# Cluster-masked attention: centroid products in four column tiles, one-hot rows made on two engines and moved by four transfers, two weight loads moved

## Chip, cores and metric

The kernel runs on one core of one Trainium2 chip. The metric is the device time in microseconds (us), the median of three runs. TensorE is called PE, VectorE DVE, ScalarE ACT, GpSimd POOL and SyncE SP, as in the profile.

## What is computed

Attention in which a query sees only the keys of its own cluster, followed by two mixture-of-experts layers (8 experts, width 512, hidden 1024, 1536 tokens). The change touches the attention alone, and two loads of the first layer's weights.

```python
B, H, S, D = 2, 8, 768, 64; n_clusters = 16
q_assign = argmax(q_n @ c_n^T); k_assign = argmax(k_n @ c_n^T)     # normed rows and centroids
mask = q_assign[:, :, :, None] == k_assign[:, :, None, :]
scores = scale * np.matmul(q, k.transpose(0, 1, 3, 2))
scores = np.where(mask, scores, -1000000000.0)
attn = np.exp(scores - max); attn = attn / (sum + 1e-09)
x = np.matmul(attn, v); x = moe(x); return moe2(x)
```

## The kernel before, in words

**Tiling.** Heads are worked two at a time: two batches with four head pairs each are eight "pairs", numbered 0 to 7. A pair has 12 chunks: six blocks of 128 queries for each of its two heads (j). Each chunk is a slot of the main loop, numbered 0 to 11 in its pair.

**Scores and mask.** q and k are split into a rounded part and a rest (qh, ql, kh, kl; scale folded into q), and the products run in a rounded 32-bit form. The first operands x1, y1 hold qh over ql and kh twice; the second, x2, y2, hold qh and kl in 64 rows, and from row 64 on 16 one-hot rows of the cluster of each query (values 0, 1) and of each key (values -2^100, 0). So the second product adds 0 where the clusters agree and -2^100 where they don't. The second operands stand in two sets, for even and odd pairs.

**A slot** issues, in this order: four products into a score tile pss (L238; two such tiles), its row maximum nm on DVE (L246), the six transposes ppt of the chunk two back (L268) in two tiles of three, copied to pt by ACT and DVE (L270); what is due of the products with v (av, L280, slots 10, 0, 4 and 6; px, the norm and the gate's lp at slots 1 and 7, L307 to L323); a step of preparation for the next pair; a step of other work; the exponential pe on ACT with its sum (L254). The instructions of an engine run in the order in which this loop issues them. The tiles ppt, plog, plt, poh, px and pws (products for the first layer's weight scales) share a pool of three PSUM banks.

**Preparation of the next pair** is a list of nine steps, one a slot: qh on ACT; ql on DVE, kh on ACT and kl on POOL; the products of q and k with the centroids (plog: two halves of 384 columns, each in two column tiles for q and k; lt, one half copied by ACT, one by DVE); six transposes plt; the row maximum and eq on DVE, times a rank on POOL, and the twelve transfers of operands by SP; first (m and oh on DVE: the first cluster that reaches the maximum); two empty steps; oh_t: two tiles of three transposes poh, two DVE operations that scale and shift into ot, and four SP transfers into x2 and y2. For pair 0 the list begins at slot 2, so that oh_t falls on slot 9. The q, k and v of the pair after next are loaded by SP at slots 7, 8 and 9.

**EARLY** is a table that hangs steps of the first expert layer on slots of pairs 6 (-2) and 7 (-1): "load" is a 1 MB transfer of raw weights, "piece" a step that casts them (wh on ACT L840, wl on DVE L847).

Of the kernel before, what the change touches and what calls it, by code (L numbers as in the profile page):

```python
# [15 lines left out]
BIG = float(2.0 ** 100)  # L16
WARM = 8
P0 = 2
LD = {7: "q", 8: "k", 9: "v"}
WARM2 = 6  # L20


# [6 lines left out]
def attention(tc, end, ps_t, ident, wu, q, k, v, centroids, wg, x_half, lg_sb, consts, before_half, after_half, extra, slot):  # L29


    nc = tc.nc
# [10 lines left out]
    with ExitStack() as ctx:  # L43
# [11 lines left out]
        def cpy(dst, src):  # L55
            nc.sync.dma_start(dst.bitcast(F32), src.bitcast(F32))

        def centroid_norms():

            nc.vector.tensor_tensor(c_sq, cw, cw, op=ALU.mult)  # L60
            p = ps_t.tile([P, 512], F32, tag="t", name="pc")[:64, :NP]
            for hp in range(NP):
                for t in range(2):
                    nc.tensor.matmul(p[32 * t:32 * t + 2 * G, hp:hp + 1], c_sq[:, hp].rearrange("p j g -> p (j g)"),
                                     ones, start=True, stop=True)
            nc.scalar.sqrt(c_n, p)
            nc.vector.tensor_scalar_add(c_n, c_n, 1e-6)
            nc.vector.reciprocal(c_n, c_n)
# [5 lines left out]
        def zero_rows(s):  # L74
            for j in range(2):
                for nm in ("x2", "y2"):
                    nc.gpsimd.memset(xs[nm, s, j][64:128].bitcast(F32), 0.0)
# [8 lines left out]
        def gate_loads(wgv):  # L86
            for j in range(2):
# [2 lines left out]

        cw = one.tile([P, NP, 2, G], F32, name="cw")
        c_sq = one.tile([P, NP, 2, G], F32, name="c_sq")
        c_n = one.tile([64, NP], F32, name="c_n")
        ones = one.tile([P, 1], F32, name="a_ones")
        rev = one.tile([P, G], F32, name="rev")
        msc = one.tile([64, 2], F32, name="msc")
        rw = end.tile([P, NP, P + 2 * E], F32, name="rw")
        xs = {(nm, s, j): one.tile([P, S], F32R, name=f"{nm}_{s}{j}")
              for s in range(2) for j in range(2) for nm in ("x2", "y2")}

        warm0 = one.tile([1, 1], F32, name="warm0")
        st = {}
# [41 lines left out]
            cpy(xs["y2", s, j][:D], d["kl"][r])  # L144

        def logits(pi):
            b, hp = pairs[pi]
            d = st[pi]
            d["lt"] = lt = w1.tile([64, S], F32, tag="lt", name="lt")
            for hf in range(2):  # L150
                p = ps_t.tile([P, 512], F32, tag="t", name="plog")[:64, :W]
                for t, nm in enumerate("qk"):
                    nc.tensor.matmul(p[32 * t:32 * t + 2 * G], cw[:, hp].rearrange("p j g -> p (j g)"),
                                     d[nm][:, hf * W:(hf + 1) * W], start=True, stop=True)
                if hf == 0:
                    nc.scalar.mul(lt[:, :W], p, c_n[:, hp:hp + 1])
                elif pi == 0:
                    nc.scalar.mul(lt[:, W:], p, c_n[:, hp:hp + 1])
                else:
                    nc.vector.tensor_scalar_mul(lt[:, W:], p, c_n[:, hp:hp + 1])  # L160

        def logits_t(pi):
            d = st[pi]
            p = ps_t.tile([P, 512], F32, tag="t", name="plt")[:, :C * 4 * G]
            d["lg"] = p.rearrange("p (c t j g) -> p c t j g", c=C, t=2, j=2)
            for c in range(C):
                nc.tensor.transpose(p[:, c * 4 * G:(c + 1) * 4 * G], d["lt"][:, c * P:(c + 1) * P], ident[:64, :64])
# [18 lines left out]

        def oh_t(pi):
            d = st[pi]
            ot = w1.tile([64, S], F32R, tag="lt", name="ot")
            ohv = d["oh"].rearrange("p (c i) g -> p c (i g)", i=4)  # L190
            for hf in range(2):
                p = ps_t.tile([P, 512], F32, tag="t", name="poh")[:64, :W]
                for c in range(HALF):
                    nc.tensor.transpose(p[:, c * P:(c + 1) * P], ohv[:, hf * HALF + c], ident)
                nc.vector.tensor_scalar(ot[:, hf * W:(hf + 1) * W], p, msc[:, 0:1], msc[:, 1:2],
                                        op0=ALU.mult, op1=ALU.add)
            s = pi % 2
            for j in range(2):
                cpy(xs["x2", s, j][64:64 + G], ot[j * G:(j + 1) * G])
                cpy(xs["y2", s, j][64:64 + G], ot[(2 + j) * G:(3 + j) * G])  # L200

        def first_mask(j):

# [15 lines left out]
        def first_rows(j):  # L219
            for hf in range(2):  # L220
                p = ps_t.tile([P, 512], F32, tag="t", name="poh")[:64, :W]
                for c in range(HALF):
                    nc.tensor.transpose(p[:, c * P:(c + 1) * P],
                                        oh0[j][:, hf * HALF + c].rearrange("p t g -> p (t g)"), ident)
                hs = slice(hf * W, (hf + 1) * W)
                nc.scalar.copy(xs["x2", 0, j][64:64 + G, hs], p[:G])
                nc.vector.tensor_scalar(xs["y2", 0, j][64:64 + G, hs], p[2 * G:3 * G], BIG, -BIG,
                                        op0=ALU.mult, op1=ALU.add)
# [117 lines left out]
        def last():  # L346
# [1 line left out]
            yield from after_half(B - 1, 1, rows)  # L348

        prep = [  # L350
            lambda i: part(i, "qh"),
            lambda i: (part(i, "ql"), part(i, "kh"), part(i, "kl")),
            lambda i: logits(i),
            lambda i: logits_t(i),
            lambda i: (argmax(i), operands(i, 0), operands(i, 1)),
            lambda i: first(i),
            lambda i: None,
            lambda i: None,
            lambda i: oh_t(i),
# [16 lines left out]
        zero_rows(0)  # L376
        for j in range(2):
            nc.gpsimd.memset(oh0[j], 0.0)
        for (p0, c0, x) in ((0, 0, 1.0), (0, 1, 0.0), (32, 0, BIG), (32, 1, -BIG)):
            nc.vector.memset(msc[p0:p0 + 32, c0:c0 + 1], x)  # L380
        keep_warm(WARM)
        part(0, "qh")
        centroid_norms()
# [46 lines left out]
        for i in range(len(seq) + LAG + 1):  # L430
# [15 lines left out]
            if cur:  # L446
                pi = cur[0]
                sl = i % n
                if sl in LD:
                    load(pi + 2, LD[sl])  # L450
                if i == 0:
                    for _ in masks[1]:
                        pass
                if i == 1:
                    first_rows(1)
                ps = sl - P0 + (sl - P0 > 6) if pi == 0 else sl
                if pi + 1 < NPR and 0 <= ps < len(prep):
# [267 lines left out]
class MoE:  # L725
# [353 lines left out]
    def run(self, task):  # L1079
# [3 lines left out]
        for i, u in enumerate(units):  # L1083
# [888 lines left out]
```

## Time and profile before

| | us |
|---|---|
| runs | 616.56, 616.71, 619.94; median 616.71 |
| profiled execution | 615.39 |
| its span | 613.5 |
| PE busy | 565.1 (92%) |
| DVE busy | 466.1 (76%) |
| ACT busy | 421.3 (69%) |
| POOL busy | 215.4 (35%) |

The profile shows one execution. Its time is 1.9 us above the span, which reaches from the first to the last instruction. A PE row's duration is modelled, and rows overlap; the distance from one start to the next says how long the work takes. Pair 0 begins at 12.70 us, pair 1 at 41.39, pair 7 at 234.40; the attention's last products are done by about 288, and the rest is the two expert layers.

### The profile page before, as it was taken

To read this page: it belongs to the slowest core of one execution; us is meant where nothing else is said; L and a number is where in the kernel's file an instruction comes from. 1 tells how busy PE (TensorE), PEld (TensorE's weight loads), DVE (VectorE), ACT (ScalarE), POOL (GpSimd) and SP (SyncE) were. 2 spreads that over 40 slices of the span, in tenths; PEclk is the share of its full clock that TensorE was granted. 3 is DMA by queue.
4 is the path that set the end of the run, shared out by engine and by line. 5 is a ranking of instruction groups with operands and counts; after the bars stand their busy time and mean duration, and the time that the engine had idled before them with its cause. 6 is when DMAs were issued, how large, how long until landed. Compare 5 with 4: busy or idle time off the path is not lost.

```text
span 613.5 us, 14527 instructions
## 1 busy us (share of the span) xinstructions
PE 565.1 (92%) x5428; PEld 466.1 (76%) x5428; DVE 466.1 (76%) x1186; ACT 421.3 (69%) x901; POOL 215.4 (35%) x426
## 2 busy tenths in 40 slices
PE   6899999998999998988899999997998999999993
PEld 2666767676767676657778998996887988999992
DVE  5867686778989676868586788789778666989881
ACT  4766666776676668963585787875864576969781
POOL 8702020202341110115634355624624523263441
PEclk9899999999999999999899999999999999999997
DMA  5879482747409881522466765976973657999930
GB/s 145 212 217 283 123 176 88 169 110 153 146 22 241 247 242 35 178 70 107 150 219 236 244 208 201 306 246 194 326 234 89 235 181 245 316 305 312 318 114 21
DMA packets 75920, 117.55 MB, mean 192 GB/s; under 512 B 10906, under 2 KB 43802, under 8 KB 75843
## 3 DMA queue, kind: packets, MB, share of 16 engines
q1 hardware_dynamic: 72419, 106.76, 58.3%
q0 software_dynamic: 3264, 9.72, 4.7%
q8 instruction: 45, 0.74, 0.5%
q14 instruction: 32, 0.26, 0.1%
q10 hardware_dynamic: 160, 0.07, 0.0%
HBM read 84.28 MB, written 12.87 MB: 158 GB/s over the span
## 4 chain that ended last, share of the span: by engine, by line
PE 61%; DVE 17%; ACT 12%; issue 4%; DMA 3%; SPq 1%; ACTq 0%; POOL 0%; DVEq 0%
PE ph L950 15%; PE py L1025 13%; PE av L280 9%; PE pss L238 7%; PE ppt L268 6%; PE pz L1000 3%; DVE nm L246 3%; DVE wl L847 3%; ACT wh L840 3%; ACT pe L254 2%; PE pyo L1646 2%; PE pxt L927 2%; ACT pt L270 1%; ACT xo L1700 1%; DVE hl L962 1%
## 5 line engine op out<-in xcount | busy, mean ns | idle before, releaser
L847 DVE SCALAR_TENSOR_TENSOR wl<-raw,sw,wh 128x1024 f16<-128x1024 f32 x128 | 163.5, 1284 | 17.9 <-ACT wh L840 16.8
L840 ACT ACTIVATE wh<-raw,sw 128x1024 f16<-128x1024 f32 x128 | 146.0, 1148 | 2.5 <-DMA x<-ot 2.4
L246 DVE TENSOR_REDUCE nm<-pss 128x1 f32<-128x768 f32 x96 | 91.5, 953 | 41.2 <-PE pss L238 37.6
L254 ACT ACTIVATE pe<-pss,nm 128x768 f32<-128x768 f32 x96 | 87.1, 907 | 24.2 <-DVE nm L246 24.2
L950 PEld LDWEIGHTS <-wh 128*128 128x128 f16 x1152 | 87.7, 99 | 15.4 <-issue 10.9
L238 PE MATMUL pss<-y,x 128*128 128x384 f32 x384 | 93.6, 365 | 4.8 <-ACT pe L254 3.2
L268 PE MATMUL ppt<-ident,pe 128*128 128x128 f32 x576 | 80.4, 275 | 3.3 <-ACT pt L270 1.4
L238 PEld LDWEIGHTS pss<-y,x 128*128 128x128 f32 x384 | 63.2, 190 | 25.2 <-issue 13.2
L270 ACT COPY pt<-ppt 128x384 f32<-128x384 f32 x128 | 57.9, 482 | 29.4 <-PE ppt L268 29.1
L268 PEld LDWEIGHTS ppt<-ident,pe 128*128 128x128 f32 x576 | 69.2, 142 | 8.9 <-ACT pt L270 2.3
L1025 PEld LDWEIGHTS <-wh 128*128 128x128 f16 x960 | 73.2, 100 | 3.4
L950 PE MATMUL ph<-xh,wh 128*128 128x192 f16 (+14 forms) x576 | 67.2, 240 | 8.6 <-DVE hl L962 6.2
L280 PE MATMUL av<-pt,v 128*64 128x384 f32 x384 | 68.8, 494 | 0.0
L950 PE MATMUL ph<-xl,wh 128*128 128x192 f16 (+14 forms) x576 | 67.3, 240 | 0.2 <-issue 0.2
L950 PE MATMUL ph<-xh,wl 128*128 128x192 f16 (+14 forms) x576 | 67.3, 240 | 0.0
L952 ACT ACTIVATE hh<-ph 128x128 f16<-128x128 f32 (+14 forms) x144 | 44.5, 315 | 27.1 <-PE ph L950 25.8
L962 DVE SCALAR_TENSOR_TENSOR hl<-ph,hh 128x192 f16<-128x192 f32 (+14 forms) x127 | 41.1, 336 | 24.4 <-ACT hh L952 22.8
L1025 PE MATMUL py<-hh,wh 128*128 128x192 f16 (+13 forms) x480 | 47.3, 241 | 0.5 <-ACT hh L952 0.3
L1025 PE MATMUL py<-hl,wh 128*128 128x192 f16 (+13 forms) x480 | 46.9, 240 | 0.2 <-DVE hl L962 0.2
L950 PEld LDWEIGHTS <-wl 128*128 128x128 f16 x576 | 45.5, 99 | 1.9
L1025 PE MATMUL py<-hh,wl 128*128 128x192 f16 (+13 forms) x480 | 46.7, 241 | 0.0
L280 PEld LDWEIGHTS av<-pt,v 128*64 128x64 f32 x384 | 24.8, 136 | 28.4 <-issue 28.1
(326 smaller groups left out, 865.3 us busy)
## 6 DMA issues: line engine op xcount, KB each, us to landing
raw<-in_moe_w SPq DMA_DIRECT2D x64, 1024.0 KB, 5.9
y<-kh SPq DMA_DIRECT2D x31, 192.0 KB, 4.0
x<-qh SPq DMA_DIRECT2D x30, 192.0 KB, 4.6
q<-in_q SPq DMA_DIRECT2D x8, 384.0 KB, 4.8
k<-in_k SPq DMA_DIRECT2D x8, 384.0 KB, 5.0
x<-ql SPq DMA_DIRECT2D x16, 192.0 KB, 3.3
v<-in_v SPq DMA_DIRECT2D x8, 384.0 KB
out<-zt SPq DMA_DIRECT2D x1, 3072.0 KB
```

The lines of the kernel that those rows point to most:

```text
L238: nc.tensor.matmul(p[:, hf, :W], xx[:, c * P:(c + 1) * P], yy[:, hf * W:(hf + 1) * W], start=a, stop=o)
L246: nc.vector.tensor_reduce(nm, p[:, :, :W], axis=AX.XY, op=ALU.max, negate=True)
L254: nc.scalar.activation(pe, p[:, :, :W], AF.Exp, bias=d["nm", c, j], scale=1.0, accum_out=d["sm"][:, c, j:j + 1])
L268: nc.tensor.transpose(p[:, kc * P:(kc + 1) * P], pe[:, kh, kc * P:(kc + 1) * P], ident)
L270: eng(pt[:, kh * HALF:(kh + 1) * HALF, (c % HALF) * P:(c % HALF + 1) * P], p.rearrange("p (a b) -> p a b", a=HALF))
L280: nc.tensor.matmul(p[j * D:(j + 1) * D, :W], d["v"][:, j, kc, :], d["pt", hf, j][:, kc, :], start=(kc == 0), stop=(kc == C - 1))
L840: nc.scalar.activation(hi[:, :, s], x[:, :, s], AF.Copy, scale=sw)
L847: nc.vector.scalar_tensor_tensor(lo[:, :, s], x[:, :, s], sw, hi[:, :, s], op0=ALU.mult, op1=ALU.subtract, accum_out=fl)
L950: nc.tensor.matmul(p[:, :N], w[:, c, fs], x[:, c, :N], start=(k == 0), stop=(k == 11))
L952: nc.scalar.activation(hh[:, f, :N], p[:, :N], AF.Relu)
L962: nc.vector.scalar_tensor_tensor(hl[:, f, :N], p[:, :N], 0.0, hh[:, f, :N], op0=ALU.max, op1=ALU.subtract)
L1025: nc.tensor.matmul(p[:, :N], w[:, f, s], x[:, f, :N], start=(k == 0), stop=(k == 23))
```

## The change

1. **plog** is one tile of 128 partitions: q and k, first and second half, in four column tiles; lt is one operation, on DVE (ACT for pair 0). plt is three transposes of 128 rows instead of six of 64, and so is poh.
2. **The rows.** DVE makes oa (both kinds of rows, two heads' worth of partitions), and POOL multiplies it twice by a factor 0 or 1 for each partition (own) into ot, so that rows of the other head are zero for k. x2 and y2 of both heads are one tile, and each of the four transfers fills 32 rows of both heads: oa for x2 goes to both heads, ot to y2.
3. **Steps.** Preparation has eight steps: logits at slot 0; plt and qh; argmax, kh and kl; ql; first and the operands' transfers; two empty; oh_t at slot 7 (slot 9 for pair 0, as before). The loads of q and k stand behind oh_t in the same slot, v one slot later.
4. **EARLY.** The third and fourth load of raw weights move from slots 4 and 6 of pair 6 to slots 8 and 10. At the start, the memsets of msc move from DVE (four) to POOL (eight), and DVE sums the identity into own.

```diff
-LD = {7: "q", 8: "k", 9: "v"}
+LD = {7: "qk", 8: "v"}
...
-                for t in range(2):
+                for t in range(4):
                     nc.tensor.matmul(p[32 * t:32 * t + 2 * G, hp:hp + 1], c_sq[:, hp].rearrange("p j g -> p (j g)"),
                                      ones, start=True, stop=True)
...
-        xs = {(nm, s, j): one.tile([P, S], F32R, name=f"{nm}_{s}{j}")
-              for s in range(2) for j in range(2) for nm in ("x2", "y2")}
+        xs2 = {(nm, s): one.tile([P, 2, S], F32R, name=f"{nm}_{s}") for s in range(2) for nm in ("x2", "y2")}
+        xs = {(nm, s, j): t[:, j] for (nm, s), t in xs2.items() for j in range(2)}
...
         def logits(pi):
-            d["lt"] = lt = w1.tile([64, S], F32, tag="lt", name="lt")
+            d["lt"] = lt = w1.tile([P, W], F32, tag="lt", name="lt")
+            p = ps_t.tile([P, 512], F32, tag="t", name="plog")[:, :W]
             for hf in range(2):
-                p = ps_t.tile([P, 512], F32, tag="t", name="plog")[:64, :W]
                 for t, nm in enumerate("qk"):
-                    nc.tensor.matmul(p[32 * t:32 * t + 2 * G], cw[:, hp].rearrange("p j g -> p (j g)"),
+                    r = 64 * hf + 32 * t
+                    nc.tensor.matmul(p[r:r + 2 * G], cw[:, hp].rearrange("p j g -> p (j g)"),
                                      d[nm][:, hf * W:(hf + 1) * W], start=True, stop=True)
-                if hf == 0:
-                    nc.scalar.mul(lt[:, :W], p, c_n[:, hp:hp + 1])
-                elif pi == 0:
-                    nc.scalar.mul(lt[:, W:], p, c_n[:, hp:hp + 1])
-                else:
-                    nc.vector.tensor_scalar_mul(lt[:, W:], p, c_n[:, hp:hp + 1])
+            if pi == 0:
+                nc.scalar.mul(lt, p, c_n[:, hp:hp + 1])
+            else:
+                nc.vector.tensor_scalar_mul(lt, p, c_n[:, hp:hp + 1])
...
-            for c in range(C):
-                nc.tensor.transpose(p[:, c * 4 * G:(c + 1) * 4 * G], d["lt"][:, c * P:(c + 1) * P], ident[:64, :64])
+            for c in range(HALF):
+                nc.tensor.transpose(p[:, c * P:(c + 1) * P], d["lt"][:, c * P:(c + 1) * P], ident)
...
         def oh_t(pi):
             d = st[pi]
-            ot = w1.tile([64, S], F32R, tag="lt", name="ot")
-            ohv = d["oh"].rearrange("p (c i) g -> p c (i g)", i=4)
+            oa = w1.tile([P, W], F32R, tag="lt", name="oa")
+            ot = w1.tile([P, 2, W], F32R, tag="ot", name="ot")
+            ohv = d["oh"].rearrange("p (c i) g -> p c (i g)", i=8)
+            p = ps_t.tile([P, 512], F32, tag="t", name="poh")[:, :W]
+            for c in range(HALF):
+                nc.tensor.transpose(p[:, c * P:(c + 1) * P], ohv[:, c], ident)
+            nc.vector.tensor_scalar(oa, p, msc[:, 0:1], msc[:, 1:2], op0=ALU.mult, op1=ALU.add)
+            for j in range(2):
+                nc.gpsimd.tensor_scalar(ot[:, j], oa.bitcast(F32), own[:, j:j + 1], None, op0=ALU.mult)
+            s = pi % 2
             for hf in range(2):
-                p = ps_t.tile([P, 512], F32, tag="t", name="poh")[:64, :W]
-                for c in range(HALF):
-                    nc.tensor.transpose(p[:, c * P:(c + 1) * P], ohv[:, hf * HALF + c], ident)
-                nc.vector.tensor_scalar(ot[:, hf * W:(hf + 1) * W], p, msc[:, 0:1], msc[:, 1:2],
-                                        op0=ALU.mult, op1=ALU.add)
-            s = pi % 2
-            for j in range(2):
-                cpy(xs["x2", s, j][64:64 + G], ot[j * G:(j + 1) * G])
-                cpy(xs["y2", s, j][64:64 + G], ot[(2 + j) * G:(3 + j) * G])
+                cpy(xs2["x2", s][64:96, :, hf * W:(hf + 1) * W],
+                    oa[64 * hf:64 * hf + 32].unsqueeze(1).to_broadcast([32, 2, W]))
+            for hf in range(2):
+                cpy(xs2["y2", s][64:96, :, hf * W:(hf + 1) * W], ot[64 * hf + 32:64 * hf + 64])
...
         prep = [
-            lambda i: part(i, "qh"),
-            lambda i: (part(i, "ql"), part(i, "kh"), part(i, "kl")),
             lambda i: logits(i),
-            lambda i: logits_t(i),
-            lambda i: (argmax(i), operands(i, 0), operands(i, 1)),
-            lambda i: first(i),
+            lambda i: (logits_t(i), part(i, "qh")),
+            lambda i: (argmax(i), part(i, "kh"), part(i, "kl")),
+            lambda i: part(i, "ql"),
+            lambda i: (first(i), operands(i, 0), operands(i, 1)),
             lambda i: None,
             lambda i: None,
             lambda i: oh_t(i),
...
+        for j in range(2):
+            nc.vector.tensor_reduce(own[:, j:j + 1], ident.rearrange("p (a i g) -> p a i g", i=2, g=G)[:, :, j],
+                                    axis=AX.XY, op=ALU.add)
...
-                if sl in LD:
-                    load(pi + 2, LD[sl])
...
-                ps = sl - P0 + (sl - P0 > 6) if pi == 0 else sl
+                ps = sl - P0 if pi == 0 else sl
                 if pi + 1 < NPR and 0 <= ps < len(prep):
                     prep[ps](pi + 1)
+                for nm in LD.get(ps, ()):
+                    load(pi + 2, nm)
...
-         (-2, 4): ('load',),
-         (-2, 6): ('load',),
+         (-2, 8): ('load',),
          (-2, 9): ('open_ring', 'open_first', 'piece'),
-         (-2, 10): ('gather',),
+         (-2, 10): ('gather', 'load'),
```

Three places show how instructions move; the names are the program's tiles. First SP's queue at the end of pair 1, where the transfers of the second operands (x2 and y2 of the odd set, before x_10, x_11, y_10, y_11, after x_1 and y_1) and the loads stand. Before:

```order
L56 DMA y_1221<-kh 64x768 x2
L56 DMA x_1220<-ql 64x768
L56 DMA x_11_171<-qh 64x768
L56 DMA y_11_172<-kl 64x768
L1400 DMA wsm<-in_moe_w 128x8x64
L114 DMA q<-in_q 128x768
L114 DMA k<-in_k 128x768
L56 DMA x_10_169<-ot 16x768
L56 DMA y_10_170<-ot 16x768
L56 DMA x_11_171<-ot 16x768
L56 DMA y_11_172<-ot 16x768
L111 DMA v<-in_v 128x768
```

and after the change:

```order
L56 DMA x_1211<-qh 64x768
L56 DMA y_1212<-kh 64x768 x2
L56 DMA x_1211<-ql 64x768
L56 DMA x_1_168<-qh 64x768
L56 DMA y_1_169<-kl 64x768
L1408 DMA wsm<-in_moe_w 128x8x64
L56 DMA x_1_168<-oa 32x2x384 x2
L56 DMA y_1_169<-ot 32x2x384 x2
L115 DMA q<-in_q 128x768
L115 DMA k<-in_k 128x768
L112 DMA v<-in_v 128x768
```

The loads of q and k stood ahead of the rows' transfers and now stand behind them.

Second, DVE's queue in slots 1 to 4 of pair 1, from the norm's ri on (after the change from the end of slot 0). Before:

```order
L295 TENSOR_SCALAR ri<-sm 128x6
L296 RECIPROCAL ri<-ri 128x6
L315 TENSOR_TENSOR lp<-px,ri 128x48
L323 TENSOR_TENSOR x<-px,ri 128x3x128
L124 SCALAR_TENSOR_TENSOR ql<-q,qh 128x768
L246 TENSOR_REDUCE nm<-pss 128x1
L270 COPY pt_762<-ppt 128x3x128
L160 TENSOR_SCALAR lt<-plog,c_n 64x384
L246 TENSOR_REDUCE nm<-pss 128x1
L270 COPY pt_791<-ppt 128x3x128
L246 TENSOR_REDUCE nm<-pss 128x1
L270 COPY pt_762<-ppt 128x3x128
```

and after:

```order
L161 TENSOR_SCALAR lt<-plog,c_n 128x384
L252 TENSOR_REDUCE nm<-pss 128x1
L301 TENSOR_SCALAR ri<-sm 128x6
L302 RECIPROCAL ri<-ri 128x6
L321 TENSOR_TENSOR lp<-px,ri 128x48
L329 TENSOR_TENSOR x<-px,ri 128x3x128
L252 TENSOR_REDUCE nm<-pss 128x1
L276 COPY pt_766<-ppt 128x3x128
L176 TENSOR_REDUCE mx<-plt 128x24
L178 TENSOR_TENSOR eq<-plt,mx 128x384
L252 TENSOR_REDUCE nm<-pss 128x1
L276 COPY pt_795<-ppt 128x3x128
```

lt has moved ahead of nm of slot 1, mx and eq from slot 4 to slot 2, and ql from slot 1 to slot 3.

Third, ACT's queue from the end of pair 0's last products to slot 4 of pair 1. Before:

```order
L270 COPY pt_950<-ppt 128x3x128 x2
L287 COPY avo<-av_1024 128x384
L122 ACTIVATE qh<-q 128x768
L254 ACTIVATE pe,sm<-pss,nm 128x768
L270 COPY pt_992<-ppt 128x3x128 x2
L126 CAST kh<-k 128x768
L254 ACTIVATE pe,sm<-pss,nm 128x768
L270 COPY pt_1127<-ppt 128x3x128
L156 ACTIVATE lt<-plog,c_n 64x384
L254 ACTIVATE pe,sm<-pss,nm 128x768
L270 COPY pt_1163<-ppt 128x3x128
L254 ACTIVATE pe,sm<-pss,nm 128x768
```

and after:

```order
L276 COPY pt_959<-ppt 128x3x128 x2
L293 COPY avo<-av_1016 128x384
L260 ACTIVATE pe,sm<-pss,nm 128x768
L276 COPY pt_986<-ppt 128x3x128 x2
L123 ACTIVATE qh<-q 128x768
L260 ACTIVATE pe,sm<-pss,nm 128x768
L276 COPY pt_1124<-ppt 128x3x128
L127 CAST kh<-k 128x768
L260 ACTIVATE pe,sm<-pss,nm 128x768
L276 COPY pt_1160<-ppt 128x3x128
L260 ACTIVATE pe,sm<-pss,nm 128x768
L276 COPY pt_1124<-ppt 128x3x128
```

qh has moved from slot 0 into slot 1 and kh from slot 1 into slot 2; ACT's half of lt is gone.

## Rows read from the trace of the kernel before

**Rows 1.** Busy time by stretch, pair 1: us, PE, PEld, DVE, ACT, POOL, clock, DMA.
```profile
41.39:72.12 30.73, 30.38 (x203) 22.00 (x202) 22.05 (x40) 20.47 (x45) 3.61 (x6) 1.00 0.78 220
```

**Rows 2.** PE's timeline in pair 1: start, duration, operation, count; stretches of one kind joined.
```profile
45.02 0.97 PE L238 MATMUL pss<-y,x 128*128 128x384 f32 x4
...
47.29 0.97 PE L238 MATMUL pss<-y,x 128*128 128x384 f32 x4
48.10 0.82 PE L268 MATMUL ppt<-ident,pe 128*128 128x128 f32 x6
48.84 0.51 PE L153 MATMUL plog<-q,cw 128*32 128x384 f32 x1
...
50.81 0.97 PE L238 MATMUL pss<-y,x 128*128 128x384 f32 x4
...
52.88 0.97 PE L238 MATMUL pss<-y,x 128*128 128x384 f32 x4
...
56.52 0.97 PE L238 MATMUL pss<-y,x 128*128 128x384 f32 x4
...
57.90 0.96 PE L238 MATMUL pss<-y,x 128*128 128x384 f32 x4
...
61.52 0.97 PE L238 MATMUL pss<-y,x 128*128 128x384 f32 x4
...
63.63 0.96 PE L238 MATMUL pss<-y,x 128*128 128x384 f32 x4
```

**Rows 3.** Groups by line and form, 41.39 to 234.4 us: busy us, mean ns, idle before.
```profile
L246 DVE TENSOR_REDUCE nm<-pss 128x1 f32<-128x768 f32 x73 | 69.6, 953 | 33.4 <-PE pss L238 30.4 <-ACT pe L254 1.9 <-ACT qh L122 0.8
L254 ACT ACTIVATE pe<-pss,nm 128x768 f32<-128x768 f32 x72 | 65.3, 907 | 18.2 <-DVE nm L246 18.2
...
L270 ACT COPY pt<-ppt 128x384 f32<-128x384 f32 x96 | 43.6, 481 | 27.4 <-PE ppt L268 27.1
...
L254 ACT ACTIVATION_READ_ACCUMULATOR pe<-pss,nm 128x1 f32 x72 | 14.4, 201 | 0.0
...
L1483 POOL TENSOR_SCALAR x<-x,sx 128x512 f32<-128x512 f32 x6 | 9.3, 1574 | 0.0
L195 DVE TENSOR_SCALAR ot<-poh,msc 64x384 fp32r<-64x384 f32 x12 | 7.5, 658 | 0.0
L323 DVE TENSOR_TENSOR x<-px,ri 128x384 f32<-128x384 f32 x12 | 6.6, 549 | 0.0
L177 POOL TENSOR_TENSOR eq<-eq,rev 128x384 f32<-128x384 f32 x6 | 6.1, 1013 | 29.8 <-DVE eq L176 17.2 <-DVE sw L1418 6.4 <-DVE rx L689 4.2
...
L122 ACT ACTIVATE qh<-q 128x768 fp32r<-128x768 f32 x6 | 5.1, 849 | 0.0
...
L315 DVE TENSOR_TENSOR lp<-px,ri 128x48 f32<-128x48 f32 x12 | 2.5, 208 | 1.2
L296 DVE RECIPROCAL ri<-ri 128x6 f32<-128x6 f32 x12 | 2.3, 192 | 0.4
```

**Rows 4.** PE's waits from 12 to 235 us: total, times, longest.
```profile
PE plog L153 <- ACT pt L270: 3.6, 6, 1.4
...
PE pss L238 <- DMA y<-ot: 1.1, 1, 1.1
```

**Rows 5.** PE's timeline at the second layer's gate product, 341 to 343 us.
```profile
341.73 0.72 PE L1675 MATMUL pq<-yt,wgc 128*32 128x304 f32 x8
342.38 0.38 PE L1042 MATMUL pq<-flt,ones 128*128 128x1 f32 x2
```

**Rows 6.** DVE's timeline at 36 us, in pair 0.
```profile
36.37 1.24 DVE L195 TENSOR_SCALAR ot<-poh,msc 64x384 fp32r<-64x384 f32 x2
```

**Rows 7.** DMA issues, 41 to 235 us: count, KB each, median us to landing.
```profile
q<-in_q SPq DMA_DIRECT2D x5, 384.0 KB, 4.8
...
x<-ot SPq DMA_DIRECT2D x12, 48.0 KB, 4.2
y<-ot SPq DMA_DIRECT2D x12, 48.0 KB, 2.1
```

More of the change, by code (lines that the diff above doesn't have):

```diff
@@ L60, in centroid_norms @@
             nc.vector.tensor_tensor(c_sq, cw, cw, op=ALU.mult)
-            p = ps_t.tile([P, 512], F32, tag="t", name="pc")[:64, :NP]
+            p = ps_t.tile([P, 512], F32, tag="t", name="pc")[:, :NP]
             for hp in range(NP):
-                for t in range(2):
+                for t in range(4):
                     nc.tensor.matmul(p[32 * t:32 * t + 2 * G, hp:hp + 1], c_sq[:, hp].rearrange("p j g -> p (j g)"),
@@ L92, in attention @@
         c_sq = one.tile([P, NP, 2, G], F32, name="c_sq")
-        c_n = one.tile([64, NP], F32, name="c_n")
+        c_n = one.tile([P, NP], F32, name="c_n")
         ones = one.tile([P, 1], F32, name="a_ones")
         rev = one.tile([P, G], F32, name="rev")
-        msc = one.tile([64, 2], F32, name="msc")
+        msc = one.tile([P, 2], F32, name="msc")
+        own = one.tile([P, 2], F32, name="own")
         rw = end.tile([P, NP, P + 2 * E], F32, name="rw")
-        xs = {(nm, s, j): one.tile([P, S], F32R, name=f"{nm}_{s}{j}")
-              for s in range(2) for j in range(2) for nm in ("x2", "y2")}
+        xs2 = {(nm, s): one.tile([P, 2, S], F32R, name=f"{nm}_{s}") for s in range(2) for nm in ("x2", "y2")}
+        xs = {(nm, s, j): t[:, j] for (nm, s), t in xs2.items() for j in range(2)}
         warm0 = one.tile([1, 1], F32, name="warm0")
@@ L223, in first_rows @@
                     nc.tensor.transpose(p[:, c * P:(c + 1) * P],
-                                        oh0[j][:, hf * HALF + c].rearrange("p t g -> p (t g)"), ident)
+                                        oh0[j][:, 2 * c + hf].rearrange("p t g -> p (t g)"), ident)
                 hs = slice(hf * W, (hf + 1) * W)
@@ L378, in attention @@
             nc.gpsimd.memset(oh0[j], 0.0)
-        for (p0, c0, x) in ((0, 0, 1.0), (0, 1, 0.0), (32, 0, BIG), (32, 1, -BIG)):
-            nc.vector.memset(msc[p0:p0 + 32, c0:c0 + 1], x)
         keep_warm(WARM)
@@ L409, in attention @@
         zero_rows(1)
+        for j in range(2):
+            nc.vector.tensor_reduce(own[:, j:j + 1], ident.rearrange("p (a i g) -> p a i g", i=2, g=G)[:, :, j],
+                                    axis=AX.XY, op=ALU.add)
+        for p0 in (0, 64):
+            for (p1, c0, x) in ((0, 0, 1.0), (0, 1, 0.0), (32, 0, BIG), (32, 1, -BIG)):
+                nc.gpsimd.memset(msc[p0 + p1:p0 + p1 + 32, c0:c0 + 1], x)
         consts()
```

## The prediction

> **What bounds the kernel now.** I read the span cut at the starts of the head pairs first: in pair 1, 30.73 us long, TensorE (PE) is busy 30.38, DVE 22.05 and ACT 20.47 [rows 1]. The attention stage is bound by PE, but "busy" includes the gaps of a pipelined engine, so the next view is PE's timeline of that pair, slot by slot [rows 2]. A slot is one chunk: four products, six transposes of an earlier chunk, and what is due; it reaches from one pss row with a full set to the next. A bare one takes 1.38 us (56.52 to 57.90). Then I read the durations by line [rows 3], to see which queue comes second behind PE, and PE's waits [rows 4], which name the buffer or transfer that PE stood at.
>
> **Part 1: less work on PE.** The slot with the logits takes 3.52 us (47.29 to 50.81 [rows 2]), 2.14 more than a bare one. Part of it is a wait: the second half's products need a bank that ACT must first empty; 3.6 us of such waits stand in six places [rows 4]. In four column tiles there is one bank and the eight passes go side by side. The nearest rows are eight passes of a later product with 32 columns each: from 341.73 to the next matmul at 342.38 are 0.65 us at 304 columns [rows 5], which is 0.82 at 384 if all of it scales, and less if a part is fixed. I take 0.78. Bounds: 0.65, and 1.37 if they ran two by two as now (48.84 to 50.81 is 1.97, less a mean wait of 0.6).
>
> The Trainium skill, "TensorE: Matmul & The Clock Gate", section "Measured speedup vs the span model", gives 2.38 times for three column tiles, four fifths of ideal. By that the products would take about 1.0, an estimate, and the preparations would give back some 1.5 us of the sum. The row of eight passes speaks for nearly full overlap.
>
> The six transposes of the logits make their slot 0.69 longer than a bare one (50.81 to 52.88 is 2.07). Six of 128 rows take 0.74 (48.10 to 48.84), so three take 0.37. The one-hot rows fall from six to three too. PE saves 2.14 - 0.78 + 0.69 - 0.37 + 0.74 - 0.37 = 2.05 us in each of seven preparations: 14.4 us if nothing else binds.
>
> **Part 2: what takes it back.** There are two score buffers, so a chunk's products wait for the exponential two chunks back. Its path is products 0.81 (47.29 to 48.10), nm 0.95, exp 0.91 [rows 2, 3]. Where a slot has no av, a late nm or exp shows at once.
>
> Slots 1 to 3 now have a PE floor of 2.27 (slot 1 with px, 45.02 to 47.29) + 0.37 + 2 x 1.38 = 5.4 us. On ACT stand, from slot 1 on, pt 0.48, qh 0.85, exp 0.91 and the reading of its sum 0.20, two pt, kh as long as qh, exp again: 5.4 us in rows that overlap by about 0.1 each, so 4.5; they begin 1.3 after slot 1 does, since ACT needs the products and three transposes. That is 5.8, so +0.4. Before, qh stood in slot 0, under av, which hid it.
>
> Slots 7 to 9 have a floor of 2.11 (61.52 to 63.63) + 0.37 + 2 x 1.38 = 5.24. On DVE stand nm, pt, the norm's four (two of 0.2 or less, 0.21, 0.55), then oa, and only then nm of slot 8 with its exp: 5.8 by the same way of summing, so +0.55. For oa I take the row of ot, 0.66 [rows 3]: the same length on more lanes. The second ot of 0.66 is saved, but in slot 8, where it was hidden.
>
> A clean pair (1) thus gains 2.05 - 0.4 - 0.55 = 1.1 us. Pair 0, 1.0. Pair 2, 0.45: a product of the weight scales takes a bank in slot 2, so that the transposes of slot 3 wait for eq on DVE, +0.65. Pair 3, 1.2: the same, but 0.75 of waits at ACT's pt go. Pair 4, 1.9: 0.8 of such waits go. Pair 5, 0.6: POOL's three scalings (1.57 each [rows 3]) now stand ahead of eq and kl there, which I price at 0.5. Pair 6, 2.4: 1.3 in its preparation, and its first products stood 1.1 us at a row of y [rows 4], which is now made a slot earlier. Pair 7 and both experts' stages, 0: the two moved weight loads have pair 7 to land in. The kernel's start, 0: two small sums on DVE against four memsets that leave it.
>
> **Part 3: the rows' new path.** Before, DVE wrote ot and SP copied it. Now DVE makes oa, POOL two ot, and SP issues four transfers and only then q and k. For POOL's 128x384 with a factor per partition the rows give 1.01 (eq, the same shape with two tensors) and 1.18 (the scaling, 1.57 at 512, by size) [rows 3]. I take 1.01, as ot reads one tensor. Bounds 0.7 and 1.6.
>
> The Trainium skill, "GPSIMD Engine Reference", section "4.1 Engine selection", sends elementwise work to VectorE and calls one-input work on GpSimd roughly line-rate. By it an ot would take about DVE's 0.66, an estimate, and the chain would be 0.7 shorter; POOL's scaling row, which has one tensor too, speaks against that.
>
> In a normal pair oa ends about 4.0 us after slot 7 starts (the DVE sum above up to oa), the ot at 6.0; the two y transfers leave by 7.2, at 0.6 each, and land 2.1 (y rows) to 4.2 us (x rows) later [rows 7]: I take 9.6 to 10.3. The next pair's second products need them at 5.24 + 0.55 + 1.38 + 3.63 (slots 10 and 11, 3.63 being the slot with av, 57.90 to 61.52, that stands at 10) + 0.4 = 11.2. Covered by about 1 us. q and k leave at 7.2 and 8.2, land 4.8 later [rows 7], at 12.0 to 13.2; the logits behind av in slot 0 want them at about 14.4. Covered by about 1 us, and what stands behind a plog that waits is the whole of PE, and DVE and ACT behind it.
>
> From pair 0 to pair 1 that cover is missing, since preparation runs two slots later there. oa starts where ot did, at 36.37 [rows 6], and ends at 37.0, the ot at 39.1, the last y transfer leaves at 39.8 and lands, at 3.4 (near the middle of 2.1 and 4.2), at 43.2; pair 1's second products would come at 41.39 [rows 1] + 0.4 - 1.0 = 40.8. PE waits 2.4 us. Bounds 1 and 4.
>
> Sum: -1.0 + 2.4 - 1.1 - 0.45 - 1.2 - 1.9 - 0.6 - 2.4 = -6.2 us. The profiled execution, 615.39, becomes 609.2; the median of the runs, 616.71, is 1.3 above it, so 610.5.
>
> **Rivals.**
> 1. The floor holds: ACT's and DVE's queues fit, since their rows overlap more than I say. Then -14.4 + 2.4 - 1.1 (pair 6's wait) is -13.1, and with the waits in pairs 3 and 4 that I counted apart -14.6: 602 to 604. For it: neither engine is busy three quarters of a pair [rows 1]. Against it: both sums say 5.8, and the products start no earlier than exp lets them.
> 2. Taken back whole: in pairs 1, 4, 5 and 6 a bank wait comes like that of pairs 2 and 3 (0.65 x 4 = 2.6), and the column tiles stay at 1.37 (0.6 x 7 = 4.1). Then -6.2 + 6.7, about 0: 616 to 617. Against the second half: rows 5.
> 3. Slower: POOL's ot takes 1.6 us and the transfers land 1 us later than the rows say. At y that is 1.2 + 1 less the cover of 1, so 1.2; behind it q and k lose 0.9 more; 2.1 at six pair starts is 12.6: -6.2 + 12.6 is 623.1. It decides from an ot of about 1.5 or a landing 1 us later. For it: x rows took 4.2 for 48 KB, and their bytes double. Against it: no POOL row by size is above 1.2.
>
> **Numbers.** The forecast, -3 to -9, 0.50; rival 1, 0.18; rival 2, 0.20; rival 3, 0.12. A measurement of this kernel tells about 1% from no change, so the borders are 610.5 and 622.9. The forecast lies on the first, so half of it counts as faster: 0.25 + 0.18 = 0.43; same 0.25 + 0.20 = 0.45; slower 0.12. The range, 602 to 619, leaves out rival 3 and the last part of rival 1.
>
> **What will show it.** Right: eight plog passes in one group and 0.78 us from them to the next PE row; three plt and three poh; pair 1 at 29.6 us besides its first wait; a PE wait of about 2.4 at a transfer of ot at pair 1's start and none at pairs 2 to 7; POOL's ot near 1.0. Wrong: such a wait at each pair's start (rival 3), plog at 1.37 or ppt waits in every slot 3 (rival 2), slots 1 to 3 at 5.4 and 7 to 9 at 5.2 (rival 1).

## The result, and the profile after

The changed kernel takes 610.02 us (median of four runs, 608.49 to 610.97), the kernel before 617.58 in the runs beside it: ratio 0.988, 95% interval 0.984 to 0.991, so a gain of a little over 1%, clear of no change. One run of a kernel further below (rows at slot 6, 616.92 us) was of a slower kind, over 1.5% above that kernel's fastest, and is left out of its time. The profiled execution takes 609.18 against 615.39. Forecast were 610.5 and 609.2. The sum was met and the terms were not all met, which is the subject of what follows.

The page of the changed kernel, span and busy time of PE and its weight loads and the other engines:

```profile
span 607.3 us, 14459 instructions
...
PE 556.0 (92%) x5399; PEld 460.1 (76%) x5399; DVE 466.9 (77%) x1177; ACT 416.1 (69%) x893; POOL 231.5 (38%) x448
```

The span cut at the starts of pairs 1 to 6, columns as in [rows 1]:

```profile
41.08:72.82 31.74, 29.77 (x197) 21.44 (x196) 22.88 (x39) 19.90 (x44) 6.65 (x8) 1.00 0.86 247
72.82:103.14 30.32, 29.40 (x200) 21.69 (x199) 23.14 (x43) 20.36 (x45) 6.21 (x8) 1.00 0.61 146
103.14:133.82 30.68, 29.88 (x201) 21.69 (x199) 23.99 (x48) 23.09 (x57) 6.19 (x8) 1.00 0.60 146
133.82:166.43 32.61, 30.80 (x199) 22.00 (x200) 27.39 (x70) 22.32 (x58) 11.22 (x11) 1.00 0.57 142
166.43:198.54 32.11, 30.05 (x206) 21.80 (x204) 28.76 (x72) 20.19 (x46) 11.36 (x11) 1.00 0.59 158
198.54:230.22 31.68, 29.50 (x197) 21.47 (x195) 24.19 (x45) 21.20 (x46) 7.50 (x9) 1.00 0.75 204
```

Pair 1 is 1.0 longer than in [rows 1]. Term by term, a pair's length from its first products to the next pair's (the kernel before: 30.73, 31.05, 31.76, 33.60, 31.91 and 33.95 for pairs 1 to 6):

| | predicted | measured |
|---|---|---|
| start of pair 0; pair 0 | 0; -1.0 | +0.9; -1.2 |
| pair 1, its first wait included | +1.3 | +1.0 |
| pair 2; pair 3 | -0.45; -1.2 | -0.7; -1.1 |
| pair 4; pair 5 | -1.9; -0.6 | -1.0; +0.2 |
| pair 6 | -2.4 | -2.3 |
| pair 7 and the experts | 0 | -2.0 |
| sum | -6.2 | -6.2 |

At pair 7's start the change has gained 4.2 us, 2.0 less than forecast. The other 2.0 come later, where nothing was changed: about 1.0 while the granted clock of the kernel before was 0.97 (400 to 460 us) and that of the changed one 1.00, and 0.9 behind the last weight cast, a stretch that took 20.6 to 22.1 us in the profiled executions of this study, whatever was changed. The start of pair 0 lay between 12.46 and 13.65 in kernels with the same code before it. Pair 0 itself, -1.2 in the table, lasted 28.9 in the kernel with the old EARLY (below), whose code is the changed kernel's up to pair 6, and 27.5 here, so its term is not told from chance. Pairs 1 to 5 agree within 0.05 us each in these two kernels. So I compare pairs 1 to 6 below: 193.0 us before, 189.2 after.

PE's timeline of pair 1 after the change, to be read beside [rows 2]:

```profile
41.08 0.60 PE L244 MATMUL pss<-y,x 128*128 128x384 f32 x2
42.40 0.98 PE L244 MATMUL pss<-y,x 128*128 128x384 f32 x2 [0.72 <-issue]
...
46.05 0.51 PE L156 MATMUL plog<-q,cw 128*32 128x384 f32 x1
...
46.83 0.97 PE L244 MATMUL pss<-y,x 128*128 128x384 f32 x4
...
49.03 0.49 PE L169 MATMUL plt<-ident,lt 128*128 128x128 f32 x3
49.28 0.95 PE L244 MATMUL pss<-y,x 128*128 128x384 f32 x4
...
52.75 0.97 PE L244 MATMUL pss<-y,x 128*128 128x384 f32 x4 [0.40 <-ACT pe L260]
...
56.39 0.97 PE L244 MATMUL pss<-y,x 128*128 128x384 f32 x4
...
58.50 0.97 PE L244 MATMUL pss<-y,x 128*128 128x384 f32 x4 [0.49 <-ACT pe L260]
```

From 46.05 to 46.83 are the eight passes, in 0.78 us; plt adds no more than 0.25 (49.03 to 49.28). The first wait is at 42.40, at y's rows (their last transfer is issued at 40.7 and takes 2.2 to land). Slots 1 to 3 last 5.92 (46.83 to 52.75). Slot 5 (56.39 to 58.50) lasts 2.11 instead of the bare 1.38; that wait for exp was not in the forecast. The same pair on the other engines:

```profile
53.92 1.82 POOL L129 TENSOR_TENSOR kl<-k,kh 128x768 fp32r<-128x768 f32 x1
54.05 2.50 DVE L125 SCALAR_TENSOR_TENSOR ql<-q,qh 128x768 fp32r<-128x768 f32 x1
...
56.48 0.94 DVE L252 TENSOR_REDUCE nm<-pss 128x1 f32<-128x768 f32 x1
...
57.46 0.90 ACT L260 ACTIVATE pe<-pss,nm 128x768 f32<-128x768 f32 x1 [2.39 <-DVE nm L252]
```

ql on DVE, 0.95 us by itself, takes 2.50. It begins 0.13 after kl on POOL and ends 0.8 after kl does. nm of the next chunk stands behind it, exp behind nm (2.39 idle), and the products of slot 6 behind exp.

### The profile page after: what moved, and what is told of

Same layout as the page of the kernel before. It is cut to its first block, busy times and chain, and to the rows that moved or that the text cites. A ratio compares the mean times of both kernels' runs of the same rounds, so it can differ in the third digit from the quotient of the medians.

```text
span 607.3 us, 14459 instructions
## 1 busy us (share of the span) xinstructions
PE 556.0 (92%) x5399; PEld 460.1 (76%) x5399; DVE 466.9 (77%) x1177; ACT 416.1 (69%) x893; POOL 231.5 (38%) x448
## 4 chain that ended last, share of the span: by engine, by line
PE 61%; DVE 19%; ACT 9%; DMA 4%; issue 3%; POOL 2%; SPq 0%; ACTq 0%; DVEq 0%; POOLq 0%
PE ph L959 15%; PE py L1034 13%; PE av L286 9%; PE pss L244 8%; PE ppt L274 5%; DVE nm L252 4%; PE pz L1009 3%; ACT pe L260 3%; DVE wl L856 3%; ACT wh L849 2%; PE pyo L1654 2%; PE pxt L936 1%; DVE ql L125 1%; DMA xg<-x2d,idx2a 1%; PE plog L156 1%
## 5 line engine op out<-in xcount | busy, mean ns | idle before, releaser
L252 DVE TENSOR_REDUCE nm<-pss 128x1 f32<-128x768 f32 x96 | 91.2, 951 | 28.0 <-PE pss L244 27.5
L1909 POOL DMA_INDIRECT out<-xo,tk x16 | 20.7, 1292 | 67.1 <-ACT xo L1902 16.6
```

The costliest lines, as they stand in the source:

```text
L252: nc.vector.tensor_reduce(nm, p[:, :, :W], axis=AX.XY, op=ALU.max, negate=True)
```

## The experiments

Each edit is one to the changed kernel, unless another is named. Ratios are to the kernel before in runs beside each; the runs are from four chips, so ratios are compared and not times. The profiles are read at the same places, so that a difference of a few tenths in a pair can be told, which the total can't.

**kl ahead of ql.**

```diff
-            lambda i: (logits_t(i), part(i, "qh")),
-            lambda i: (argmax(i), part(i, "kh"), part(i, "kl")),
+            lambda i: (logits_t(i), part(i, "kh"), part(i, "kl")),
+            lambda i: (argmax(i), part(i, "qh")),
```

> The changed kernel with kh and kl one step earlier (slot 1) and qh one step later (slot 2), so that POOL's kl is done before DVE's ql begins. Theory: DVE's ql takes 2.50 us instead of 0.95 because it stands still until POOL's kl ends; nm of the next chunk is then late and the products of slot 6 wait about 0.6. Then here ql is back near 0.95, slot 5 falls from 2.05 to 2.11 to about 1.4 in pairs 1, 4 and 6, and pair 7 begins 2.5 to 3.5 us earlier than its 230.22 of the changed kernel; total about 607. Rival (ql is long for its own place, with the operands' transfers reading and writing the same memory): ql stays at 2.5 and pair 7 begins at 230 as now.

607.49 us, 0.984 [0.981, 0.988]; pairs 1 to 6 last 187.5. The groups by line, columns as in [rows 3]:

```profile
L129 POOL TENSOR_TENSOR kl<-k,kh 128x768 fp32r<-128x768 f32 x6 | 11.0, 1834 | 12.2 <-ACT kh L127 12.2
...
L125 DVE SCALAR_TENSOR_TENSOR ql<-q,qh 128x768 fp32r<-128x768 f32 x6 | 5.7, 948 | 0.0
```

ql's mean falls from 1.92 us to 0.95, and slot 5 is 1.38 again in pairs 1 and 6. The theory holds in its mechanism. Its size was too large: pair 7 begins 2.4 earlier, but 1.0 of that is an earlier start of pair 0, and pairs 1 to 6 gain 1.7. Pair 4 lost 0.8, where PE's transposes now wait for DVE's pt. By the rows the cause is the same neighbour in another place. These are POOL's and DVE's rows in pair 4 with kl first, and the last is the same copy in the changed kernel:

```profile
139.53 1.84 POOL L129 TENSOR_TENSOR kl<-k,kh 128x768 fp32r<-128x768 f32 x1 [12.15 <-ACT kh L127]
140.00 1.40 DVE L1460 COPY pre<-base 128x8 f32<-128x8 f32 x1
...
142.02 0.16 DVE L1460 COPY pre<-base 128x8 f32<-128x8 f32 x1
```

A copy of 8 columns, part of the other work in that slot, takes 1.40 us instead of 0.16 and ends with kl.

**qh back under av, as well.** The edit is shown against the kernel with kl first.

```diff
-            lambda i: logits(i),
-            lambda i: (argmax(i), part(i, "qh")),
+            lambda i: (logits(i), part(i, "qh")),
+            lambda i: argmax(i),
```

> As the kernel with kl first, and qh in slot 0 beside av, where it stood before the change. Theory: besides ql's wait, ACT's queue in slots 1 and 2 makes the 0.56 us wait of slot 3 in pairs 1 and 6 and part of pair 4's 0.92; with qh under av these go. Pair 7 begins 4.5 to 6 us earlier than 230.22, so at 224.5 to 226, total 604 to 606. Rival (slot 3 waits for nm on DVE, whose queue has mx and eq there, not for ACT): no more than the kernel with kl first, 227 to 228.

607.40 us, 0.984 [0.981, 0.988]; pairs 1 to 6 186.8. Slot 3 of pair 1 falls from 2.05 to 1.67, so ACT's queue was 0.4 of its wait, as the prediction had it, and the rest is DVE's: exp stands there for nm. Pair 6 gains as much and pair 4 nothing. The size of the theory was missed: pair 7 began at 227.07, within the rival's bounds.

**Rows at slot 6.**

```diff
             lambda i: None,
-            lambda i: None,
             lambda i: oh_t(i),
+            lambda i: None,
```

> The changed kernel with oh_t one slot earlier (slot 6, beside av; slot 8 in pair 0), loads where they were. Theory: oa on DVE ahead of nm of slot 8 costs the 0.40 to 0.49 us that slot 9 waits in pairs 1 to 4 and 6, and the lateness of POOL's ot costs the 1.25 us in which pair 1's first products stand. Then both go: five times 0.4 and 1.2, pair 7 begins 3 to 3.5 us earlier, at 227, total about 607. Rival (oa only moves: now nm of slot 7 is late and slot 8 waits as much, while the first products of pair 1 wait for something else): pair 7 begins at 229 to 230.

607.48 us (three runs), 0.988 [0.982, 0.993]; pairs 1 to 6 187.6, and pair 7 begins at 228.8 and not at 227. Slot 9 goes on waiting 0.5 in pairs 1 to 3 and 6 without oa in slot 7: nm, the norm and nm again stand there. But it is not the same wait: the norm's ri takes 0.41 to 0.48 us there instead of 0.16, beside POOL's ot, so that about 0.3 of it is new, and what oa cost in slot 7 stays open. What was gained stands at pair 1's first wait (0.6) and in pair 6 (1.4: the first weight cast no longer waits).

**The column tiles.** Two tiles of PSUM, and then the same with both in column tiles 0 and 1. The edit shown is the second's; the first keeps r and all 128 partitions of each tile. In both, ACT makes half of lt and DVE half, as before the change.

```diff
-            p = ps_t.tile([P, 512], F32, tag="t", name="plog")[:, :W]
             for hf in range(2):
+                p = ps_t.tile([P, 512], F32, tag="t", name="plog")[:64, :W]
...
-                    r = 64 * hf + 32 * t
+                    r = 32 * t
```

> The changed kernel with the logits in two PSUM tiles of two column tiles each, one half of lt on ACT and one on DVE, as before the change. Theory: the four column tiles are worth their difference on PE wherever they stand: slot 0 grows from 4.41 by 0.58 (1.36 against 0.78) in six pairs, and by a bank wait of up to 0.5; pair 7 begins 3.5 to 7 us later, at 234 to 237, total 613 to 617. Rival (the step's move to slot 0, beside av, is what removed the cost, and other queues set the slots behind it): pair 7 begins within 1 us of 230.2.

> The changed kernel with the logits in two PSUM tiles whose products both stand in column tiles 0 and 1 (the run before this used two tiles, but kept four column positions, and its slot 0 stayed at 4.40). Theory: the column positions decide, not the bank: slot 0 becomes 3.63 + 1.36 = 5.0 in pairs 2 and 6 instead of 4.41, and pairs 1 to 6 together last 3 to 3.5 us longer than the changed kernel's 189.2, about 192.5. Rival (the products overlap whatever their position, and what cost time before the change was only the wait for the bank): slot 0 stays at 4.4.

With two banks and four positions: 612.48 us, 0.992 [0.990, 0.995], but slot 0 stays at 4.40 and pairs 1 to 6 at 189.8; most of the rest lies in pair 0 (29.1), whose length differs by itself. Pair 7 begins at 232.2, between theory and rival. The edit did not undo what I meant to undo. With positions 0 and 1 twice: 618.80 us, 1.000 [0.997, 1.003], pairs 1 to 6 193.3, slot 0 5.03. PE's timeline in pair 2:

```profile
80.51 0.51 PE L156 MATMUL plog<-q,cw 128*32 128x384 f32 x1
...
81.18 0.49 PE L156 MATMUL plog<-q,cw 128*32 128x384 f32 x1
...
81.92 0.97 PE L245 MATMUL pss<-y,x 128*128 128x384 f32 x4
```

Half the passes start 0.67 later, and to the next products are 1.41 us instead of 0.78. The two kernels differ in the position alone. So the position makes the passes go side by side, not the bank, and without it pairs 1 to 6 last 3.5 us more, as long as before the change.

**ot on DVE** (`nc.vector.tensor_scalar` for `nc.gpsimd.tensor_scalar`).

> The changed kernel with ot made by DVE instead of POOL. Theory: DVE's queue in slot 7 sets slot 10, so two more operations ahead of nm of slot 8 come on top of the 0.4 that slot 9 waits now: 0.7 to 1.3 a pair, pairs 1 to 6 together 4 to 8 us longer than 189.2, while the wait at pair 1's start shrinks from 1.25 to about 0.5. Rival (DVE does them in 0.3 each and has room there): within 1.5 us of 189.2.

A single run: 615.18 us, pairs 1 to 6 191.7. Neither size was met: DVE makes an ot in 0.42 us, POOL in 1.25, and the 0.84 a pair on DVE cost 1.1 in pair 2 and gave 0.9 back at pair 1's start. POOL, three times slower, was the better place, because nobody waits for it in a pair with cover.

**The old EARLY.**

```diff
-         (-2, 8): ('load',),
+         (-2, 4): ('load',),
+         (-2, 6): ('load',),
...
-         (-2, 10): ('gather', 'load'),
+         (-2, 10): ('gather',),
```

> The changed kernel with the third and fourth load of raw weights at slots 4 and 6 of pair 6 as before. Theory: these loads have pair 7 to land in, either way; pair 6 stays within 0.3 of 31.69 and the first weight cast within 0.5 us of 227.76. Rival (at slots 4 and 6 they stand on the queues ahead of the rows' transfers, so the first cast, which waits for a transfer of rows, and with it slot 11 of pair 6 come later): pair 6 is longer by 0.5 or more.

A single run: 621.82 us. Pair 6 lasts 38.3 instead of 31.7, and pair 7's first slot 6.2 instead of 3.7. The timeline of this kernel at the end of pair 6, SP's queue and ACT:

```profile
220.84 1.99 SPq L822 DMA_DIRECT2D raw<-in_moe_w  x2
...
222.94 3.09 SPq L56 DMA_DIRECT2D x<-oa  x2
...
226.12 2.08 SPq L56 DMA_DIRECT2D y<-ot  x2
...
235.28 1.15 ACT L849 ACTIVATE wh<-raw,sw 128x1024 f16<-128x1024 f32 x1 [9.27 <-DMA y<-ot]
```

and of the changed kernel:

```profile
221.92 1.76 SPq L56 DMA_DIRECT2D x<-oa  x2
...
224.49 1.23 SPq L56 DMA_DIRECT2D y<-ot  x2
...
225.91 1.25 SPq L822 DMA_DIRECT2D raw<-in_moe_w  x2
...
227.76 1.15 ACT L849 ACTIVATE wh<-raw,sw 128x1024 f16<-128x1024 f32 x1 [2.64 <-issue]
```

In the new order of steps SP reaches the two raw loads only at 220.84, right ahead of the rows. The rows, 96 KB each, share the queues with 2 MB, and the first weight cast, which by the profile waits for them, begins at 235.28, after 9.3 us idle. The rival held, more than it said.

**Loads of q and k ahead of the rows.**

```diff
+                for nm in LD.get(ps, ()):
+                    load(pi + 2, nm)
                 if pi + 1 < NPR and 0 <= ps < len(prep):
                     prep[ps](pi + 1)
-                for nm in LD.get(ps, ()):
-                    load(pi + 2, nm)
```

> The changed kernel with the loads of q and k ahead of the rows' transfers on SP, as before the change. Theory: the rows have about 1 us of cover in every pair but the first, and two loads of 384 KB ahead of them on the same queues take more than that: products at the starts of pairs 2 to 6 wait 0.5 to 2 us each for ot, pair 1 another 2, pairs 1 to 6 together 193 to 200. Rival (the loads do not hold up the rows, which leave only when POOL is done, by then the loads have landed): within 1 us of 189.2.

A single run: 620.64 us, pairs 1 to 6 197.8. PE's timeline at pair 1's start, and that stretch as in [rows 1]:

```profile
41.05 0.60 PE L244 MATMUL pss<-y,x 128*128 128x384 f32 x2
45.63 0.98 PE L244 MATMUL pss<-y,x 128*128 128x384 f32 x2 [3.99 <-issue]
46.41 1.48 PE L274 MATMUL ppt<-ident,pe 128*128 128x128 f32 x6
```

```profile
41.05:52.40 11.35, 7.36 (x34) 3.47 (x32) 2.63 (x4) 2.56 (x6) 0.00 (x0) 0.70 0.97 298
```

PE stands 4.15 us in all between the two halves of one chunk's products, and works at 0.70 of its clock over the stretch, part of it at the lower of its two levels (1.2 GHz): pair 1 is 5.6 longer for 3.3 more of waiting. Pair 3 waits 1.8, pairs 4 to 6 0.3, pair 2 nothing. So the order of the rows and the loads on SP keeps waits like rival 3's away, most of all at pair 1.

**The old steps with the new tiles.**

```diff
+            lambda i: part(i, "qh"),
+            lambda i: (part(i, "ql"), part(i, "kh"), part(i, "kl")),
             lambda i: logits(i),
-            lambda i: (logits_t(i), part(i, "qh")),
-            lambda i: (argmax(i), part(i, "kh"), part(i, "kl")),
-            lambda i: part(i, "ql"),
-            lambda i: (first(i), operands(i, 0), operands(i, 1)),
+            lambda i: logits_t(i),
+            lambda i: (argmax(i), operands(i, 0), operands(i, 1)),
+            lambda i: first(i),
```

> The changed kernel's tiles, operations and transfers in the order of steps of the kernel before (qh; ql, kh and kl; logits; plt; argmax and operands; first; two empty; oh_t at slot 8, slot 10 in pair 0). Theory: the change's gain on PE is real in any order, and its own order of steps gives part of it back (POOL's kl against ql, qh out of av's cover). Then pairs 2 to 6 lose the 1.36 of plog and 0.32 of plt against the kernel before and nothing waits in slots 3 and 5: pair 2 about 29.2 to 29.5 against 31.05 before and 30.32 with the change; but pair 1 stands 3 to 4 us for its rows, and pair 6's first products wait again. Pairs 1 to 6 together 183 to 187 (193.0 before, 189.2 with the change). Rival (the new order was needed, since with the old one the latency of nm and exp, or a PSUM bank, takes the gain): 189 or more.

621.04 us, 1.006 [1.003, 1.009]. Pair 2 lasts 29.68, so the gain on PE is there; pairs 1 to 6 200.3, mostly by waits for rows at pairs 1, 3 and 6, so the theory's 183 to 187 was missed. Rows come at slot 8 here and the loads of q and k at slot 7, ahead of them on SP as in the run above; what of the waits is due to the order of steps alone, this run can't tell.

```profile
PE pss L244 <- DMA y<-ot: 4.8, 2, 3.4
PE pss L244 <- issue: 4.0, 1, 4.0
```

**The old steps with rows at slot 6** (the same list with `oh_t` one place earlier than in the changed kernel, and one empty step behind it).

> The changed kernel's tiles and transfers with the steps of the kernel before, except that oh_t comes at slot 6, beside av (slot 8 in pair 0). Theory: with the old order nothing waits in slots 3, 5 and 9 (pair 2 lasted 29.68 there against 30.32 with the change), and what made that order slow was only that its rows came at slot 8, too late for the next pair (waits of 4.2, 1.5 and 3.6 at pairs 1, 3 and 6). With the rows at slot 6 those go: pairs 1 to 6 together 182 to 185 (189.2 with the change, 196 or more where rows came at slot 8 with loads as here), total 602 to 606. Rival (rows behind the operands' transfers on SP, which this order issues later, so the first products of the next pair go on waiting): 188 or more.

606.67 us, 0.981 [0.978, 0.983]. Pairs 1 to 6 last 185.6; pairs 1, 4 and 6:

```profile
40.29:69.55 29.26, 28.96 (x197) 21.42 (x196) 21.69 (x39) 20.10 (x44) 6.07 (x8) 1.00 0.96 279
...
130.05:164.92 34.87, 32.06 (x203) 23.05 (x201) 28.05 (x70) 22.63 (x58) 11.36 (x11) 0.95 0.54 137
...
196.65:225.87 29.22, 28.98 (x198) 21.44 (x196) 21.75 (x43) 21.50 (x46) 8.27 (x9) 1.00 0.83 238
```

No wait for rows is left, and pairs 1 and 6 are 1.5 shorter than pair 1 was before. The forecasts, 182 to 185 and 602 to 606, were missed by 0.6 and 0.7 us. Pair 4 is 2.3 longer than with the change: the copy of 8 columns takes 1.79 us there, beside kl (1.77 in the kernel before), PE waits 1.6 for DVE's pt behind it, and the granted clock of the pair is 0.95.

**qh first, rows at slot 6.** Both edits on the kernel with kl first.

> The kernel with qh in slot 0 and kl ahead of ql, and its rows at slot 6. Theory: the two gains add, since they stand at different waits: pairs 1 to 6 of the first were 186.8 together, of the second 187.6, against 189.2, so here 185 to 185.5, with pair 6 at about 29.2 to 29.5 as its first weight cast no longer waits; total 604 to 606. Rival (the waits overlap, so that the second gain is hidden by the first): 186.5 or more.

608.97 us, 0.986 [0.982, 0.989]; pairs 1 to 6 185.7, pair 6 29.2: the gains nearly add (3.5 of 2.4 + 1.5). The total, forecast at 604 to 606, is not told apart from the kernel with either alone.

**The old steps, and those of the change in pair 4 alone** (a second list, taken where `pi == 4`, on the kernel with the old steps and its rows at slot 6).

> The old order with rows at slot 6, and in pair 4 alone the steps of the change (logits in slot 0, plt and qh, argmax with kh and kl, ql), rows at slot 6. Theory: DVE is the busiest of the side engines in pair 4 (28.4 of 33.6 us before the change), and with plt in slot 3 there the transposes wait for DVE's pt, so that the old order lasts 34.87 in pair 4 while the new one lasted 32.6 to 33.1; each order is right where its neighbour engines have room. Then pair 4 is 33 here and pair 7 begins 1.5 to 2 us earlier than 225.87, at 224, total about 605. Rival (what pair 4 waits for belongs to the work of other steps in it, not to the order): pair 4 stays above 34.3.

602.73 us, 0.978 [0.974, 0.982]; pair 7 begins at 223.53. Pair 4:

```profile
129.53:162.58 33.05, 30.56 (x203) 21.90 (x201) 27.72 (x70) 22.54 (x58) 11.22 (x11) 1.00 0.57 146
```

The fastest kernel here, below both that were given. Its total is not told apart from that of the old steps throughout, but pair 4 is 1.8 shorter (34.87 to 33.05), as forecast. The theory's reason, that DVE is the busiest side engine there, leaves out a row: kl now runs later in that pair, the copy of 8 columns takes 0.16 again, and the clock is 1.00. That the copy alone made the difference is not shown, since the whole list changes in pair 4.

## Why the prediction was right, and where not

- **Part 1** was right: 0.78 for the products, 0.25 for plt, 0.34 for poh (slot 7, 2.44 against 2.11). That it is the column position was argued from [rows 5] and is now shown.
- **Part 2, slots 1 to 3**: 5.8 forecast, 5.92 measured; ACT's part is shown by moving qh, the rest stays with DVE.
- **Part 2, slots 7 to 9**: 5.8 forecast, 5.65 measured (62.14 to 67.79). The reason, oa ahead of nm, is not shown: without oa there the wait stays, part of it by ri's. The same three slots took 5.6 before as well, so the 0.37 of poh was not gained there.
- **The step that failed** is the list of places where nm is late. It has slots 1 to 3 and 7 to 9; ql, which the change moves to slot 3, stands in no sum, which puts it at nothing. It measured 1.3 to 2.5 us in pairs 1 to 6 instead of 0.95, because POOL works beside it, kl above all, and slot 5 waits 0.7 for it in the clean pairs 1 and 6; with kl first that wait is gone. So a clean pair gains 0.4 (pair 6's first eleven slots, 28.94 against 29.36 without their old first wait), not 1.1, and pair 1 lasts 30.4 besides its first wait, not 29.6. The prediction prices kl on POOL's queue alone. The Trainium skill, "SBUF — State Buffer", section "Who interferes with whom", says that a DVE instruction with two inputs in SBUF contends with a GpSimd instruction that reads SBUF, and that the later one stands still until the first ends. The trace agrees: ql ends 0.8 after kl, and is 0.95 where kl comes first.
- **The step from pair 0 to pair 1**: the mechanism was right, the size was 1.35 (slot 0 of pair 1 lasts 5.76, 41.08 to 46.83, against 4.41 in pairs 2 and 6), not 2.4. I took the middle of two landing times, 3.4; and 1.01 for ot. The views by tile:

```profile
L200 POOL TENSOR_SCALAR ot<-oa,own x14: 1244/1248/1275, 37.6 to 223.2; 128x384 fp32r<-128x384 f32 x14
...
DMA to landing us min/median/max: 2.2/2.2/2.5
```

  The landing was worth 1.2, and ot 0.5 the other way. The rest: oa began 0.4 later than ot had, and the second products would have come 0.7 later than I reckoned.
- **EARLY at 0** was right as a sum (pair 7's slots are as before to 0.02) and wrong as a reason. The loads do not just have pair 7 to land in: left where they were, they stood before the rows and cost 6.6 in pair 6 and 2.5 in pair 7, in a single run. The change carried its own remedy, and I did not see the illness.
- **Pairs 4 and 5** came out 0.8 to 0.9 worse than forecast each. Slot 5 waits 0.8 and 1.2 there, behind a DVE queue with more in it than ql: small steps of the first expert layer, some of which are longer beside POOL too. In pair 4 an operation of 128x24 takes 1.01 us beside POOL's eq (0.18 alone), in pair 5 one of 128x48 takes 1.59 beside kl (0.21 alone). ql is not the cause alone, since with kl first pair 4's slot 5 waits longer (2.72 against 2.14), and in pair 5 the wait moves to slot 3 (3.67 against 2.46). How it divides is not shown.
- **Rival 3** was a real one. The covers of about 1 us held, with rows landing in 2.2; the run with the loads ahead shows what happens where they don't.
- That the total agreed to half a microsecond is luck: pairs 1 to 6 gained 3.9 where 5.3 were forecast, and 2.0 us came from later stretches that the change doesn't touch.

## What to carry to other kernels

When work moves to another engine or another slot, look at who runs beside it there and not only at what queues behind it: DVE's ql was given no cost and met POOL's kl, and kl moved out of its way met a copy of 8 columns. A change to one queue's order (SP's here) has to be followed to everything else on that queue; two loads that nobody waited for were the dearest thing in this change. Apply cheaper tiles and a new order apart: the tiles gained, and the old order with one step moved used them better.

## What was not expected of the hardware

- A PE wait of about 4 us costs more than itself: the granted clock of the stretch with it is 0.70, and PE's rows behind the wait are longer (six transposes 1.48 us instead of 0.82).
- DVE's long rows beside POOL are not only those of operations with two tensors: a copy of 128x8 took 1.40 to 1.80 us beside kl in six kernels, the one before among them, and 0.16 elsewhere.
- Rows of twice the bytes (96 against 48 KB) landed in 2.2 us, against the 2.1 to 4.2 of [rows 7].
